# Reordering the last batch and the final stores of a fused cross-attention and squared-ReLU MLP kernel on one Trainium2 core

## The chip, the cores and the metric

The kernel runs on one core of one Trainium2 chip. The metric is the device time of one execution in microseconds (us). TensorE (PE) multiplies matrices into PSUM, VectorE (DVE) and ScalarE (ACT) do element-wise work and empty PSUM, GpSimd (POOL) and SyncE (SP) mostly issue DMA transfers here. The four runs of the kernel before took between 209.67 and 211.04 us, with a median of 210.51 us.

## What is computed

Eight batches, eight heads, 512 tokens and 32 state rows a head, 64 channels. Each token reads from the state, each state row reads from the tokens, and both reads pass through a two-layer MLP with a squared ReLU:

```python
scores = scale * np.matmul(x, state.transpose(0, 1, 3, 2))
a = softmax(scores)
xread = np.matmul(a, state)                # token reads, 512 rows a head
scores2 = scale * np.matmul(state, x.transpose(0, 1, 3, 2))
a2 = softmax(scores2)
sread = np.matmul(a2, x)                   # state reads, 32 rows a head
x = concat(xread, sread) -> [B * (512 + 32), 512]
h = x @ w_in                               # 512 -> 2048
r = np.maximum(h, 0.0)
g = s * (r * r) + b
out = g @ w_out                            # 2048 -> 512
```

The inputs and the output are float32; the kernel computes with float16 operands and float32 sums. The output has 4352 rows of 512.

## The kernel before

The work of a batch is laid out as a stage of sixteen steps, f = 0 to 15, one step for each block of 128 of the 2048 hidden channels. `pieces(s)` gives what stage s does beside that, and the main loop over s and f (lines 857 to 900) puts everything in order. The order on PE, SP and POOL is the order of the program (`manual_schedule`, line 691); a scheduler places VectorE's and ScalarE's instructions, with a few held behind others by `issue_after`.

**First layer.** The state is multiplied into `w_in` beforehand, so that a batch has a matrix M, built in four blocks by `att_M`, and h is the product of M with the shares `a4`. A step's h (`mm1_x`) is two matmuls of 512 columns into one bank of the PSUM pool `psH`, which has two buffers. ScalarE applies the ReLU (line 395), VectorE squares two steps at a time (line 402). The result g is held in float16.

**Second layer.** For batches 1 to 7 the second product is computed by a scheme with seven half-size products instead of eight, whose operands are sums and differences of blocks of g (`token_sum`) and of the output weights (`weight_sums`). `fast_items(b)` lists the small matmuls of these products in an order written by hand (lines 626 to 635). An entry (p, k0, k1) stands for product p, steps k0 to k1, two matmuls of 256 columns a step. Product 1 collects in bank A, and product 2 goes on collecting in bank A once product 1 has been read out as `qa` (line 585). Product 6 collects in bank B, is read out as `u2` (line 588, `u` in the profile), and product 7 goes on in B, until `u3` (line 593), and product 4 goes on in B. Products 5 and 3 share bank C. All three come from the pool `psO`, which has two buffers. The first half of product 6 needs the token sum number 2 of steps 0 to 3, its second half that of steps 4 to 7 (line 502).

A batch's first 16 matmuls (product 1) run in its own stage, the other 96 in the next stage, seven a step. In steps 4 to 12 of stages 2 to 7 these seven stand before that step's h (line 874), in the other steps behind it.

**Beside it.** In stage s the attention of batch s+1 is made: M and the scores T at step 4 and M again at step 10, the exponential E on ScalarE, its transpose ET by a DMA on SP, the shares on VectorE, and a transpose of these back (`a4`) by a DMA. T and M need the transposed state `stT`. For batches under NST = 5 the transpose is made on PE (`att_stT`, two matmuls of 128 columns and a copy on VectorE), for the others by one DMA transpose on SP (`stT_dma`, line 160), issued in step 9 of stage 2. V, the state read, is 32 small matmuls at step 10 (`att_V`, line 338) into a bank of `psH`, scaled by ScalarE. Its transpose goes into `srdT`; for the last batch PE makes it, at step 11 (`att_srT`).

**The end.** In stage 7, whose batch is the last, `mm1_sr(i)` for the state reads joins at steps 12 to 15: four matmuls of 256 columns into a bank of `psH`. Then lines 908 to 918 run the state reads' steps 4 to 15, with five of the last batch's remaining matmuls (`rest`) behind each, and two of the state reads' own (`rows`) from step 12 on. After that come the remaining products. In the last batch products 5 and 3 are done for each of two token blocks on its own, in a bank each, and `put_last` (line 569) adds up and stores each block: 128 rows of 256 float32, 128 KB.

Of the kernel before, what the change touches and what calls it, by code (L numbers as in the profile page):

```python
# [14 lines left out]
def kernel(  # L15
# [10 lines left out]
    nc = tc.nc  # L26
# [15 lines left out]
    FC = 512  # L42
    NFC = DF // FC
    NPE = 2
    NST = 5
    NDT = 3
    NH = DM // 2
    TH = S // 2
# [289 lines left out]
    def att_V(b):  # L338
        a = A[b]
        if b >= NDT - 1:  # L340
            ps = psH.tile([P, NG, D], FP32, tag="h", name=f"V_{b}")
        else:
            ps = att_ps([P, NG, D], FP32, f"V_{b}")
        for g in range(NG):
            for c in range(SCH):
                for q in range(NQ):
                    mm(
                        ps[32 * q : 32 * q + 32, g, :],
                        a["ET"][:, SCH * g + c, 32 * q : 32 * q + 32],
                        xn[b][:, head_of(g, q), chunk_of(c), :],  # L350
                        start=(c == 0),
                        stop=(c == SCH - 1),
                        tp=(0, 32 * q),
                    )
        a["sr"] = apool.tile([P, NG, D], FP16, name=f"sr_{b}", tag="sr")
        with tc.issue_after(G["relu"]):
            for g in range(NG):
                nc.scalar.mul(a["sr"][:, g], ps[:, g], a["rq"][:, g : g + 1])
# [7 lines left out]
    def att_srT(b):  # L366
        ps = att_ps([P, NQ, Ns], FP16, f"srT_{b}")
        mm(
            ps.rearrange("p q j -> p (q j)"),
            A[b]["sr"].rearrange("p g d -> p (g d)"),  # L370
            ident16,
            is_transpose=True,
        )
        nc.vector.tensor_copy(srdT[:, b], ps)
# [131 lines left out]
    def fast_items(b):  # L506
# [62 lines left out]
        def put_last(i):  # L569
            if not ends:  # L570
                ends.append(spare("osb_last"))
            osb = ends[0][:, i]
            nc.vector.scalar_tensor_tensor(
                osb, acc["C", i], s_bc, kept["u2"][:, i], ALU.mult, ALU.add
            )
            dst = out_BSn[b, 0:S].rearrange("(q ci cj) n -> cj ci q n", ci=2, cj=2)
            nc.sync.dma_start(dst[0][i][:, NH:DM], osb)

        def blk(n0):
            return bias_bc[:, n0 : n0 + NH].unsqueeze(1).broadcast_to([P, ni, NH])  # L580
# [42 lines left out]
            elif k == 7 and i == ni - 1:  # L623
                done(p)

        order = [(1, 0, 8), (6, 0, 4), (2, 0, 3), (6, 4, 8), (2, 3, 8), (7, 0, 8)]
        order += [(5, 0, 8), (4, 0, 8), (3, 0, 8)]
        if b == last_b:
            order = [(1, 0, 8), (6, 0, 4), (2, 0, 4), (6, 4, 8), (2, 4, 5)]
            order += [(7, 0, 8), (2, 5, 8), (4, 0, 8)]  # L630
        if b == "sr":
            order = [(p, 0, 8) for p in (1, 6, 2, 7, 5, 4, 3)]
        out = [(p, k, i) for p, k0, k1 in order for k in range(k0, k1) for i in range(ni)]
# [57 lines left out]
    with tc.manual_schedule(engines={ET.PE, ET.SP, ET.Pool}):  # L691
# [90 lines left out]
        def pieces(s):  # L782
            nb = s + 1
            out = {}

            def at(f, fn):
                out.setdefault(f, []).append(fn)

            def ahead(f, fn):
                out.setdefault((f, "ahead"), []).append(fn)  # L790

            if s == 1:
                at(0, lambda: att_xT_dma(2))
                at(0, gated_x3)
                at(0, lambda: att_ET(0))
                at(0, lambda: att_ET(1))
                at(8, lambda: att_xT_dma(3))
                at(12, lambda: load_x(4))
                at(2, lambda: att_M(1, 2, "act"))
                ahead(3, bias_sum)  # L800
                at(4, bias_end)
                at(3, lambda: att_M(1, 3, "act"))
                at(6, lambda: att_stT(2))
                at(10, bias_half)
                at(8, lambda: att_M(2, 0, "act"))
                at(8, lambda: att_M(2, 1, "act"))
                at(10, lambda: att_M(2, 2, "act"))
                at(10, lambda: att_T(2, [0, 1]))
                at(11, lambda: att_ET(2))
                at(12, lambda: att_D(2, [0, 1]))  # L810
                at(13, lambda: att_M(2, 3, "act"))
                at(13, lambda: att_V(0))
                return out
            if s == 2:
                at(1, lambda: load_x(5))
            elif s in (3, 4):
                at(1, lambda: load_x(s + 3))
            if nb < B:
                if nb < NST:
                    at(0, lambda: att_stT(nb))  # L820
                ahead(4, lambda: att_M(nb, 0, "later"))
                ahead(4, lambda: att_T(nb, [0, 1]))
                ahead(4, lambda: att_M(nb, 1, "later"))
                at(4, lambda: att_ET(nb))
                at(4, lambda: A[nb]["M", 0]())
                at(6, lambda: A[nb]["M", 1]())
                at(8, lambda: att_shares(nb))
                if s in (2, 3):
                    at(6, lambda: att_xT_dma(nb + 1))
                at(9, lambda: att_a4_dma(nb))  # L830
                if s == 2:
                    at(9, stT_dma)
                elif s in (3, 4):
                    at(9, lambda: att_xT_dma(s + 3))
            if s == 2:
                at(1, lambda: att_srT_dma(0))
                at(8, lambda: att_V(1))
                at(12, lambda: att_srT_dma(1))
            ahead(10, lambda: att_V(s))
            if nb < B:  # L840
                ahead(10, lambda: att_M(nb, 2, "later"))
                ahead(10, lambda: att_M(nb, 3, "later"))
                at(10, lambda: A[nb]["M", 2]())
                at(12, lambda: A[nb]["M", 3]())
            if s == last_b:
                at(11, lambda: att_srT(s))
            else:
                at(12, lambda: att_srT_dma(s))
            if s == last_b:
                for i in range(4):  # L850
                    at(12 + i, lambda i=i: mm1_sr(i))
            return out
# [4 lines left out]
        for s in range(1, B):  # L857
            todo_s = pieces(s)
            if s in fast:
                coming[s] = fast_items(s)  # L860
            first = coming[s][:16] if s in fast else []
            if s == 1:
                items = [[] for _ in range(NKF)]
                for f in [*range(5), *range(6, 14)]:
                    items[f] = [lambda u=todo.pop(0): unit(u)]
                items[14], items[15] = first[0:8], first[8:16]
            else:
                flat = coming[s - 1][16:] + first
                n = -(-len(flat) // NKF)
                items = [flat[n * f : n * f + n] for f in range(NKF)]  # L870
            for f in range(NKF):
                for fn in todo_s.get((f, "ahead"), []):
                    fn()
                if s > 1 and 4 <= f < 13:
                    for fn in items[f]:
                        fn()
                    items[f] = []
                mm1_x(s, f)
                if s > 1 and f in (4, 5):
                    with tc.issue_after(G["last"]):  # L880
                        token_sum(s - 1, 4, f - 4)
                if s in fast:
                    if f in ((7, 9) if s == 1 else (7, 11)):
                        with tc.issue_after(G["last"]):
                            token_sum(s, 3, f // 8)
                    if s == 1 and f in (13, 14):
                        with tc.issue_after(G["last"]):
                            token_sum(s, f - 12, 0)
                    if s > 1 and f in (11, 12):
                        token_sum(s, f - 10, 0)  # L890
                    if f == 15:
                        token_sum(s, 1, 1)
                        token_sum(s, 2, 1)
                for fn in todo_s.get(f, []):
                    fn()
                if s == 1 and 5 <= f < 13:
                    with tc.issue_after(G["last"]):
                        sums.pop(0)()
                for fn in items[f]:
                    fn()  # L900
# [3 lines left out]
        def go(items, n):  # L904
            for _ in range(n):
                items.pop(0)()

        for f in range(4, NKF):
            mm1_sr(f)
            if f in (4, 5):  # L910
                token_sum(last_b, 4, f - 4)
            if f in (5, 9):
                token_sum("sr", 3, f // 8)
            if f in (11, 12, 13):
                token_sum("sr", (1, 2, 4)[f - 11], 0)
            go(rest, 5)
            if f >= 12:
                go(rows, 2)
        go(rest, 4)
# [37 lines left out]
```

## Time and profile before

| | |
|---|---|
| median of four runs | 210.51 us |
| the profiled execution | 210.34 us |
| its span, first to last instruction | 208.6 us |
| granted TensorE clock, mean | 0.994 |
| PE matmul, busy | 199.3 us (96%) |
| DVE busy | 160.0 us (77%) |
| ACT busy | 126.7 us (61%) |
| steady stages 3 to 6, from one stage's step 4 to the next one's | 21.1 us, and 21.7 once |

A stage's span holds about 21 us of PE work. PE's busy time overlaps from one matmul to the next, so a share of 96% tells that PE hardly rests, but not how much of the time it could save; for that the starts of the matmuls are compared. Waits of an engine that is ahead of PE cost nothing: ScalarE waits 46.6 us in all for h, at intervals of at most 1.4 us.

The last DMA issues and what they move, from the page: the two last stores of 128 KB on SP landed a median of 2.3 us after their issue, and the DMA transpose `stT_all`, issued at 70.8 us, landed after 4.3 us.

### The profile page before, as it was taken

What the parts mean: (1) busy time and instruction counts of PE and PEld (TensorE: products, weight loads), DVE (VectorE), ACT (ScalarE), POOL (GpSimd) and SP (SyncE); (2) the same over time, 40 slices, a digit from 0 to 9 for tenths busy, and PEclk for the clock granted to TensorE, in tenths of its full rate; (3) what the DMA queues carried; (4) which work ended last, traced back from release to release, by engine and by line L of the source; (5) the groups of instructions that cost most, each with busy time, mean ns of one, the idle gap of its engine ahead of it and who ended that gap; (6) DMA issues with size and microseconds to landing.
All of it is one profiled execution on the core that took longest, in us unless ns stands there. A gap on an engine that the chain in (4) does not pass through costs nothing.

```text
span 208.6 us, 4792 instructions
## 1 busy us (share of the span) xinstructions
PE 199.3 (96%) x1949; PEld 130.0 (62%) x1949; DVE 160.0 (77%) x275; ACT 126.7 (61%) x252; POOL 37.7 (18%) x64
## 2 busy tenths in 40 slices
PE   7988999999999999999999999999999999999991
PEld 2433343445666776677666666676667776878880
DVE  1587826979759985999579977997799787696861
ACT  3678864799477757775776567666767355533100
POOL 5970001411110231023101210210021102100210
PEclk9999999999999999999999999999999999999997
DMA  6999995999998694949752924250415012100242
GB/s 192 220 200 206 207 191 87 186 166 174 184 166 175 154 159 68 179 110 206 106 95 68 178 68 101 72 139 3 101 61 149 0 53 101 53 2 0 97 125 86
DMA packets 46491, 25.49 MB, mean 122 GB/s; under 512 B 31428, under 2 KB 44484, under 8 KB 46468
## 3 DMA queue, kind: packets, MB, share of 16 engines
q0 software_dynamic: 15536, 16.19, 40.3%
q1 hardware_dynamic: 30132, 8.62, 23.9%
q10 hardware_dynamic: 800, 0.36, 0.7%
q8 instruction: 15, 0.25, 0.5%
q14 instruction: 8, 0.07, 0.1%
HBM read 17.33 MB, written 8.91 MB: 126 GB/s over the span
## 4 chain that ended last, share of the span: by engine, by line
PE 74%; DMA 10%; DVE 8%; ACT 3%; issue 2%; POOL 0%; SPq 0%
PE h L70 21%; PE oB L70 15%; PE oC L70 10%; PE oA L70 9%; PE o L70 7%; DMA xT<-xn 5%; PE Mps L70 4%; DMA ET<-E 3%; DMA xf<-in_x_dram 3%; PE h_sr L70 2%; ACT r L395 2%; DVE g L402 2%; PE oB_sr L70 1%; PE T L70 1%; PE V L70 1%
## 5 line engine op out<-in xcount | busy, mean ns | idle before, releaser
L395 ACT ACTIVATE r<-h 128x512 f16<-128x512 f32 x126 | 74.4, 602 | 47.4 <-PE h L70 46.6
L70 PE MATMUL h<-a,M 128*128 128x512 f16 x256 | 74.2, 379 | 1.2 <-DVE M L320 0.6
L402 DVE TENSOR_TENSOR g<-r 128x1024 f16<-128x1024 f16 x64 | 43.5, 682 | 16.2 <-ACT r L395 15.6
L70 PEld LDWEIGHTS <-s 128*128 128x128 f16 x448 | 43.3, 98 | 17.5 <-DVE s L502 1.9
L70 PEld LDWEIGHTS <-g 128*128 128x128 f16 x400 | 37.6, 98 | 21.0 <-issue 5.3
L567 POOL DMA_DIRECT2D out_dram<-osb x27 | 18.2, 675 | 125.7 <-DVE osb L559 79.1
L70 PE MATMUL oB<-wd,s 128*128 128x256 f16 x224 | 32.6, 273 | 0.3 <-DVE u L588 0.2
L70 PEld LDWEIGHTS <-M 128*128 128x128 f16 x256 | 24.5, 98 | 12.9 <-issue 1.8
L70 PE MATMUL oA<-wo,g 128*128 128x256 f16 x224 | 31.7, 273 | 0.1
L297 ACT CAST M<-Mps 128x1024 f16<-128x1024 f32 x20 | 20.1, 1007 | 0.0
L70 PE MATMUL oC<-wd,s 128*128 128x256 f16 x112 | 16.5, 273 | 0.0
L70 PE MATMUL o<-wo,g 128*128 128x512 f16 x64 | 16.3, 380 | 0.0
L70 PE MATMUL oB<-wd,g 128*128 128x256 f16 x112 | 15.9, 273 | 0.0
L70 PE MATMUL oC<-wo,s 128*128 128x256 f16 x112 | 15.3, 273 | 0.0
L395 ACT ACTIVATE r_sr<-h_sr 128x256 f16<-128x256 f32 x16 | 6.1, 382 | 8.7 <-PE h_sr L70 8.7
L234 ACT ACTIVATE E<-T 128x256 f16<-128x256 f32 x20 | 7.4, 383 | 4.7 <-PE T L70 4.7
L588 DVE SCALAR_TENSOR_TENSOR u<-oB,s_bc,qa 128x512 f32<-128x512 f32 x7 | 5.3, 751 | 6.1 <-PE oB L70 6.1
L502 DVE TENSOR_TENSOR s<-s,g 128x1024 f16<-128x1024 f16 x14 | 9.6, 684 | 0.2
L70 PE MATMUL h_sr<-srdT,wi 128*128 128x256 f16 x64 | 9.6, 273 | 0.0
L496 DVE TENSOR_TENSOR s<-g 128x1024 f16<-128x1024 f16 x14 | 9.6, 684 | 0.0
L504 DVE TENSOR_TENSOR s<-g,s 128x1024 f16<-128x1024 f16 x14 | 9.6, 684 | 0.0
L500 DVE TENSOR_TENSOR s<-g,g 128x1024 f16<-128x1024 f16 x14 | 9.6, 683 | 0.0
(107 smaller groups left out, 205.6 us busy)
## 6 DMA issues: line engine op xcount, KB each, us to landing
out_dram<-osb POOLq DMA_DIRECT2D x31, 256.0 KB, 3.7
xn<-in_x_dram POOLq DMA_DIRECT2D x7, 512.0 KB, 9.4
wi<-in_moe_w_in_dram POOLq DMA_DIRECT2D x4, 512.0 KB, 8.8
wo<-in_moe_w_out_dram POOLq DMA_DIRECT2D x4, 512.0 KB, 16.4
xf<-in_x_dram SPq DMA_DIRECT2D x2, 512.0 KB, 4.6
out_dram<-osb_sr SPq DMA_DIRECT2D x8, 32.0 KB, 1.5
out_dram<-osb_sr ACTq DMA_DIRECT2D x8, 32.0 KB, 1.7
out_dram<-osb_last SPq DMA_DIRECT2D x2, 128.0 KB, 2.3
```

Of the source, the lines that this page charges most:

```text
L70: return nc.tensor.matmul(out, lhsT, rhs, start=start, stop=stop, tile_position=tp, is_transpose=is_transpose, skip_group_check=True,)
L234: nc.scalar.activation(a["E"][:, g, 256 * m : 256 * m + 256], Ts[m][:, g, :], AF.Exp, scale=scale, accum_out=a["rs"][:, NG * m + g : NG * ...
L297: nc.scalar.copy(dst, ps)
L395: nc.scalar.activation(r16[:, f % 2], hps, AF.Relu)
L402: nc.vector.tensor_mul(gt[:, f % 4 - 1 : f % 4 + 1], r16, r16)
L496: nc.vector.tensor_sub(o, a11, a21)
L500: nc.vector.tensor_add(o, a21, a22)
L502: nc.vector.tensor_sub(o, SQ[b, 1, j], a11)
L504: nc.vector.tensor_sub(o, a12, SQ[b, 2, j])
L567: nc.gpsimd.dma_start(dst[j][:, :, n0 : n0 + NH], osb)
L588: nc.vector.scalar_tensor_tensor(u, acc["B"], s_bc, kept["qa"], ALU.mult, ALU.add)
```

## The change

Six edits, in the order of the file:

- NST is 4 instead of 5: batch 4's state is transposed by the DMA too, which then moves eight blocks instead of six.
- `put_last` issues the first of the two last stores on ScalarE's queue, and the second in two halves of 64 rows, one on SP and one on ScalarE's queue.
- In ordinary batches the second product's first part, which stands between the two halves of the sixth, has four steps instead of three, and its second part four instead of five.
- In the last batch that first part has three steps instead of four; then come the sixth product's second half, three steps of the second product (instead of one), the seventh product, and the last two (instead of three).
- In stage 7 the state read V of the last batch is made ahead of step 4 instead of 10, its transpose at step 6 instead of 11, and the seven small matmuls of a step stand behind that step's h in all steps.
- In the state reads' steps 4 to 15 the number of small matmuls behind each is 4, 3, 5, 5, 5, 5, 5, 5, 5, 6, 6, 6 instead of 5 each.

```diff
-    NST = 5
+    NST = 4
...
             dst = out_BSn[b, 0:S].rearrange("(q ci cj) n -> cj ci q n", ci=2, cj=2)
-            nc.sync.dma_start(dst[0][i][:, NH:DM], osb)
+            if i == 0:
+                nc.scalar.dma_start(dst[0][i][:, NH:DM], osb)
+                return
+            for eng, p in ((nc.sync, 0), (nc.scalar, P // 2)):
+                eng.dma_start(dst[0][i][p : p + P // 2, NH:DM], osb[p : p + P // 2])
...
-        order = [(1, 0, 8), (6, 0, 4), (2, 0, 3), (6, 4, 8), (2, 3, 8), (7, 0, 8)]
+        order = [(1, 0, 8), (6, 0, 4), (2, 0, 4), (6, 4, 8), (2, 4, 8), (7, 0, 8)]
         order += [(5, 0, 8), (4, 0, 8), (3, 0, 8)]
         if b == last_b:
-            order = [(1, 0, 8), (6, 0, 4), (2, 0, 4), (6, 4, 8), (2, 4, 5)]
-            order += [(7, 0, 8), (2, 5, 8), (4, 0, 8)]
+            order = [(1, 0, 8), (6, 0, 4), (2, 0, 3), (6, 4, 8), (2, 3, 6)]
+            order += [(7, 0, 8), (2, 6, 8), (4, 0, 8)]
...
-            ahead(10, lambda: att_V(s))
+            ahead(4 if s == last_b else 10, lambda: att_V(s))
...
             if s == last_b:
-                at(11, lambda: att_srT(s))
+                at(6, lambda: att_srT(s))
...
-                if s > 1 and 4 <= f < 13:
+                if 1 < s < last_b and 4 <= f < 13:
...
-            go(rest, 5)
+            go(rest, (4, 3, 5, 5, 5, 5, 5, 5, 5, 6, 6, 6)[f - 4])
```

## The prediction

> **What bounds the kernel now.** I read the page's engine line first, then the chain of waits, then TensorE's timeline from 100 us on, matmul by matmul, and for each hole the timeline of VectorE and ScalarE beside it; last the DMA issues at the end and at 70 us.
>
> The page, engine line and the chain's shares by engine:
>
> ```profile
> PE 199.3 (96%) x1949; PEld 130.0 (62%) x1949; DVE 160.0 (77%) x275; ACT 126.7 (61%) x252; POOL 37.7 (18%) x64
> ...
> PE 74%; DMA 10%; DVE 8%; ACT 3%; issue 2%; POOL 0%; SPq 0%
> ```
>
> TensorE (PE) is the bound: three quarters of the chain is its own work. A matmul's duration on the page (273 ns for 256 columns) is longer than its slot, because matmuls overlap; start to start in one block the trace gives 109 ns for 256 columns and 216 ns for 512. With these slots a block's end is computable, and whatever lies between it and the next start is a hole. After 58 us PE loses little outside five places: one in stage 5 (batch 5, 118 to 124 us) and four in the last batch and the state-read stage. Timeline of PE, one line a block (start us, duration us, tiles, count, idle time and releaser where recorded):
>
> ```profile
> 119.33 0.59 PE L70 MATMUL h<-a,M 128*128 128x512 f16 x2
> 120.01 0.94 PE L70 MATMUL oB<-wd,s 128*128 128x256 f16 x7
> ...
> 175.45 0.60 PE L70 MATMUL h_sr<-srdT,wi 128*128 128x256 f16 x4
> 176.30 0.59 PE L70 MATMUL h<-a,M 128*128 128x512 f16 x2 [0.25 <-ACT r L395]
> ...
> 182.61 0.49 PE L70 MATMUL oB<-wd,s 128*128 128x256 f16 x3
> 183.16 0.38 PE L70 MATMUL oA<-wo,g 128*128 128x256 f16 x2
> ...
> 186.76 0.27 PE L70 MATMUL oA<-wo,g 128*128 128x256 f16 x1
> 187.22 0.60 PE L70 MATMUL oB<-wd,s 128*128 128x256 f16 x4 [0.19 <-DVE u L588]
> ...
> 191.26 0.49 PE L70 MATMUL oA<-wo,g 128*128 128x256 f16 x3
> 191.75 0.38 PE L70 MATMUL oB<-wd,g 128*128 128x256 f16 x2
> ```
>
> The reader is to see, line by line: 119.33 + 2 x 0.216 = 119.76, next start 120.01, hole 0.25; 175.45 + 4 x 0.109 = 175.89 to 176.30, 0.41; 182.61 + 0.33 = 182.94 to 183.16, 0.22; 186.87 to 187.22, 0.35; 191.59 to 191.75, 0.16. The last four add to 1.14 us.
>
> What VectorE (DVE) did at two of those holes, and the last stores:
>
> ```profile
> 182.37 0.74 DVE L585 SCALAR_TENSOR_TENSOR qa<-oA,s_bc,bias_bc 128x512 f32<-128x512 f32 x1
> 183.03 0.68 DVE L502 TENSOR_TENSOR s<-s,g 128x1024 f16<-128x1024 f16 x1
> ...
> 186.42 0.75 DVE L588 SCALAR_TENSOR_TENSOR u<-oB,s_bc,qa 128x512 f32<-128x512 f32 x1
> ...
> 203.74 1.26 SPq L577 DMA_DIRECT2D out_dram<-osb_last  x2
> 203.96 0.48 DVE L573 SCALAR_TENSOR_TENSOR osb_last<-oC,s_bc,u 128x256 f32<-128x256 f32 x1 [0.39 <-PE oC L70]
> ```
>
> qa ends at 183.11, just ahead of oA at 183.16; u ends at 187.17, just ahead of oB at 187.22. So these holes are PSUM banks being emptied.
>
> **What the Trainium skill says.** "TensorE: Matmul & The Clock Gate", section "Wait — 56ns, not 53.3ns?": a warm matmul of N columns takes N over 2.4 GHz plus about 2.5 ns from start to start, 215.7 ns for 512. The trace agrees (216, and 109 for 256). Same page, "Step-by-step: what each phase is for": matmuls stay in program order and only weight loads are pulled ahead. The trace agrees in that each hole stalls all that follows; so what counts is which matmul stands next when a bank is late. "DMA: Bandwidth & Descriptors", "Issuing engines are not separate DMA queues": two issuing queues share the same DMA engines and save only issue time. No run here shows two halves of a store yet. Same page, "Anatomy of one DMA — SWDGE (gpsimd) path": a fixed cost near 2.0 us, mostly the write's receipt, for the GpSimd path. Of the two last stores, on SP, one landed 1.9 us after its issue, the other 2.8.
>
> **The change part by part.**
>
> (1) h ahead of the products in the last batch, V at step 4, transpose at step 6. PE work is the same: the 32 V matmuls cost 0.35 us plus about 0.2 us of switching wherever they stand. In steps 4 to 12 each h comes one block of seven products (0.76 us) earlier. At step 12 the order was h(12), h_sr(0), h(13); an h bank comes free 0.43 (two h matmuls) + 0.20 + 0.60 (ScalarE's relu row) + 0.02 = 1.25 us after the h starts, and only 0.87 us of work stood between. Now h(12), h_sr(0), seven products, h(13): 1.63 us. Hole of 0.41 gone. New waits: V takes an h bank at step 4. It waits for relu(h2), done 0.06 us after h3 starts, well before V; h4 waits for relu(h3), 1.25 after h3 starts, and starts 1.66 after; h5 waits for V's two scalings (ScalarE, 0.51), done at about 2.4, and starts at 2.85. Behind the scalings on ScalarE stands relu(h4), delayed by some 0.1, and h6 wants it 1 us later. The 0.23 us copy of the state read moves forward on VectorE, where u3 behind it is wanted near 3 us after p7 ends. Cost nothing; if a cover failed, 0.1 to 0.3.
>
> (2) Last batch, 3-5 split and 3-3-2 for the second product, and 4, 3, 5 ... items a step. I count from the end of p1 (181.19 in before). oA (p2) stood 1.75 after it and waited for qa, ready at 1.97; now h_sr, 4 oB, h_sr, 3 oB, h_sr, 1 oB stand before it: 2.20. Hole 0.22 gone. The sixth product's second half wants the token sum ready at 2.52 and starts at 3.3. It ends at 4.6 (5.0 before); u waits behind other VectorE work that before ended at 5.18, so u is out at 5.9 to 6.0. The seventh product now starts at 4.6 + two h_sr + 6 oA = 6.15. Hole 0.35 gone, slack 0.2. Fourth product: the seventh now ends two small matmuls later, 1.1 us before the fourth starts, against 1.3; u3 needs 0.2 + 0.75, and VectorE now does one more small sum (0.42) before it, which the order of the built program shows. In my count that sum is done 0.3 us before the seventh product ends. Hole 0.16 gone, with only 0.1 slack. Sum of (1) and (2): 1.14 us; between 0.6 and 1.14.
>
> (3) 4-4 split in ordinary batches. Two second-product matmuls (0.22 us) go in front of the sixth product's second half, which gives its token sum that long. In stages 2, 3, 4 and 6 PE has no hole there: gain nothing. In stage 5 the hole of 0.25 shrinks to 0.03: gain 0.22. u2 comes 0.22 later; VectorE idles 0.98 us before it at 163.72, and so waits longer; behind it stand a squaring, a sum and an eviction that end 1.06 us before the next needed squaring in that stage. The seventh product follows far behind. Cost nothing; between 0 and 0.25 gain, since the stage 5 hole comes from a late transpose (ET landed 6.5 us after issue, others near 4.8) that may differ by execution.
>
> (4) NST 5 to 4. Two PE transposes (56 ns each, 0.11 us) and one VectorE copy (285 ns, beside PE) go in stage 3; stT_all grows from six blocks to eight. SP's issue of six took 1.30 us and of eight (ET, a) 1.23 to 1.26, so the queue behind it, two srdT transposes, is not moved. Landing was at 75.0; two blocks more I estimate at 4.3 x 8/6 = 5.7, so 76.5. First use is batch 4's M at 79.2. Gain 0.11.
>
> (5) Last stores. First store on ACT's queue, free at 203.72, against an issue at 203.74: no change. Second in halves on SP and ACT, both free. Fixed cost stays; the half's descriptors are out sooner (the data packets of a 128-row store ran over 0.45 us). I take 0.2. The bounds: ACT's own issue could add 0.1; the second store landed at 2.8 only because two instruction fetch packets of 8 KB (0.76 us each, at 205.3 and 205.6) lay before its last packets, and 14 of 16 engines had reported by 206.6. If the fetches fall elsewhere, 0.8 more goes.
>
> Sum: 1.14 + 0.22 + 0.11 + 0.2 = 1.67. The profiled execution took 210.34 us (span 208.57, 1.77 outside it), which gives 208.67; the median of the four runs is 0.17 higher, 210.51, so 208.84, say 208.8 us.
>
> **The rivals.**
>
> A, the waits move. VectorE has no idle time from 180.8 to 187.1, the reordering takes no work from it, and the slack I found after u and u3 is 0.2 and 0.1. For it: that saturation. Against: qa and u were each just behind PE, by 0.2 to 0.35, and are pushed past by more. Then only the 0.41, 0.11, half of (3) and of (5), and some 0.15 of (2) are gained: 0.9, 209.6 us.
>
> B, the last store misses the fetches: 0.8 more, 208.0 us. For: 14 engines on time. Against: fetches come at the end of each program, and halves use the same engines.
>
> C, slower: stT_all lands late. Batch 4's M and T now wait for that transpose. Behind it PE's whole queue waits, with E, ET and the shares for the next stage. For: the srdT transposes issued just after it took 4.1 and 5.2 us as the next x load began (75 to 79 us), and an srdT in stage 4 took 8.0. Against: 2.7 us of slack by my estimate. It costs from 79.2 on; it makes up for all the gains at a landing near 80.5 (1.2 of wait and 0.6 of VectorE backlog as in stage 4), and at 82 gives 2.8 + 0.6 - 1.6 = 1.8 slower, 212.3.
>
> That the change does nothing: not likely, as the built order shows every move.
>
> **How the numbers follow.** Forecast 0.68, A 0.18, B 0.08, C 0.06. The forecast's own range from the bounds is 208.1 to 209.3. A lies inside 209.9, so I take 207.9 to 209.8, leaving out C and tails. About 0.5% (1.05 us) is what a measurement of this kernel can tell from no change: the limit is 209.46. Forecast and B lie below it almost wholly, A mostly above: faster 0.75, same 0.19, slower 0.06.
>
> **What would show it.** h(13) starts without a ScalarE releaser; no hole above 0.05 before oA after p1, before p7 and before p4; in stage 5 the oA pair between h(2) and oB; in stage 3 no stTps, and M for batch 4 with no DMA releaser; last landing some 1.7 us earlier. I am wrong if the same holes stand before p7 or p4, if PE waits at about 79 us, or if the last landing does not follow PE's end.

## The result

The changed kernel takes 209.74 us (median of 43 runs, 208.91 to 210.84), beside 210.25 us of the kernel before (64 runs on the same chips). The ratio is 0.9975, with a 95% interval of 0.9964 to 0.9986. So it is about 0.5 us faster, where 1.67 were forecast.

The profiled execution took 209.25 us, with a span of 207.5. Its engine line and the chain's shares by engine, on its page:

```profile
PE 197.3 (95%) x1947; PEld 130.1 (63%) x1947; DVE 159.9 (77%) x274; ACT 126.8 (61%) x252; POOL 38.0 (18%) x64
...
PE 89%; DVE 3%; DMA 3%; ACT 2%; issue 0%; POOL 0%; ACTq 0%
```

PE's share of the chain has grown from 74% to 89%. Part of that is a start that went otherwise; from 58 us on it is waits that are gone from the path. Timeline of PE at the four places in the last batch and the state reads (start us, duration us, what, count):

```profile
174.85 0.60 PE L70 MATMUL h_sr<-srdT,wi 128*128 128x256 f16 x4
175.28 0.93 PE L70 MATMUL oC<-wo,s 128*128 128x256 f16 x7
176.05 0.59 PE L70 MATMUL h<-a,M 128*128 128x512 f16 x2
...
183.02 0.27 PE L70 MATMUL oB<-wd,s 128*128 128x256 f16 x1
183.13 0.60 PE L70 MATMUL oA<-wo,g 128*128 128x256 f16 x4
...
186.95 0.27 PE L70 MATMUL oA<-wo,g 128*128 128x256 f16 x1
187.06 0.60 PE L70 MATMUL oB<-wd,s 128*128 128x256 f16 x4
...
190.99 0.60 PE L70 MATMUL h_sr<-srdT,wi 128*128 128x256 f16 x4
191.43 0.82 PE L70 MATMUL oB<-wd,g 128*128 128x256 f16 x6
```

With 0.109 us a matmul every block starts where the one before it ends: 175.28 + 0.76 = 176.04, 183.02 + 0.11 = 183.13, 186.95 + 0.11 = 187.06, 190.99 + 0.44 = 191.43. All four holes are gone, and from T of batch 7 to the start of the last matmul it is 59.11 us (143.56 to 202.67) instead of 60.25 (143.40 to 203.65): 1.14 us, to the hundredth what the holes added to.

Then why only 0.5 us? Two other places of the trace after differ. The first is SP's timeline in stage 3, where the shares of batch 4 are transposed for the next stage. Before, then after:

```profile
91.13 1.24 SPq L290 DMA_TRANSPOSE a<-aT  x1
92.46 4.19 SPq L204 DMA_TRANSPOSE xT<-xn  x1
```

```profile
91.87 1.83 SPq L290 DMA_TRANSPOSE a<-aT  x1
93.80 3.61 SPq L204 DMA_TRANSPOSE xT<-xn  x1
```

The same transpose takes 0.6 us longer to issue, and by its semaphore it lands 4.31 us after its issue instead of 3.24. h of batch 4 wants it at 96.25 us; it lands at 96.18. This execution just escapes a wait. The second place is the end, in the view of the tile `osb_last`:

```profile
L578 ACTq DMA_DIRECT2D out_dram<-osb_last x1: 381/381/381, 202.8 to 202.8; - x1
L581 SPq DMA_DIRECT2D out_dram<-osb_last x1: 557/557/557, 203.5 to 203.5; - x1
L581 ACTq DMA_DIRECT2D out_dram<-osb_last x1: 583/583/583, 203.5 to 203.5; - x1
```

A half takes 557 and 583 ns to issue (a whole store 356 to 388 ns), and the halves land 2.30 and 2.59 us after their issue.

The two profiles taken alone would mislead. The start differs between executions (the first load of `stf` landed after 3.8 us in one and 5.7 us in the other, and the first T came at 6.43 and 8.05 us). From T of batch 3 to the end the one execution after is even 1.97 us shorter than the one before (148.76 and 150.73 us), more than was forecast: it escapes the wait in stage 3, and the execution before had the latest ET of stage 4 of all sixteen traces, with 0.58 us of holes behind it. The medians have to decide, and the experiments have to tell where the rest went.

### The profile page after: what moved, and what is told of

It reads as the page before. It is cut to its first block, busy times and chain, and to the rows that moved or that the text cites. A ratio compares the mean times of both kernels' runs of the same rounds, so it can differ in the third digit from the quotient of the medians.

```text
span 207.5 us, 4788 instructions
## 1 busy us (share of the span) xinstructions
PE 197.3 (95%) x1947; PEld 130.1 (63%) x1947; DVE 159.9 (77%) x274; ACT 126.8 (61%) x252; POOL 38.0 (18%) x64
## 4 chain that ended last, share of the span: by engine, by line
PE 89%; DVE 3%; DMA 3%; ACT 2%; issue 0%; POOL 0%; ACTq 0%
PE h L70 25%; PE oB L70 18%; PE oA L70 12%; PE oC L70 12%; PE o L70 7%; PE Mps L70 4%; PE h_sr L70 3%; DMA stf<-in_state_dram 3%; PE V L70 1%; PE oB_sr L70 1%; ACT r L395 1%; PE T L70 1%; DVE M L320 1%; PE oA_sr L70 1%; PE oC_sr L70 1%; PE wsum_ps L70 0%
## 5 line engine op out<-in xcount | busy, mean ns | idle before, releaser
L70 PE MATMUL oA<-wo,g 128*128 128x256 f16 x224 | 32.5, 273 | 0.0
```

Source lines behind the costliest of these rows:

```text
L70: return nc.tensor.matmul(out, lhsT, rhs, start=start, stop=stop, tile_position=tp, is_transpose=is_transpose, skip_group_check=True,)
```

## The experiments

Theory S: the split of the last store costs. Theory D: what is gained early is lost again to the pace of the transfers. Theory W: the waits of the last batch come back in most executions. After the first four runs two more: F, PE's instruction fetch has moved into the shares' transpose, and Q, the longer `stT_all` has set that transpose back. Each trace is one execution; an experiment's ratio rests on 5 to 22 runs. The times at the end of this section stand beside runs of the kernel before on the same chip.

**The parts, each alone or left out.** First the whole change without its store edit (e1), against the changed kernel:

```diff
-            if i == 0:
-                nc.scalar.dma_start(dst[0][i][:, NH:DM], osb)
-                return
-            for eng, p in ((nc.sync, 0), (nc.scalar, P // 2)):
-                eng.dma_start(dst[0][i][p : p + P // 2, NH:DM], osb[p : p + P // 2])
+            nc.sync.dma_start(dst[0][i][:, NH:DM], osb)
```

> The change with its store edit undone: both last stores whole, on SP, as in the kernel before. Theory S (the split costs: the halves landed 2.30 and 2.59 us after their issue, a whole store that no fetch packet hits about 1.95): faster than the kernel before by 1.0 to 1.4 us, ratio 0.993 to 0.995, and the last store lands near 1.9 to 2.0 us after its issue in most executions. Theory D (early gains are swallowed by the pace of the transfers, the split is neutral or a gain): ratio 0.9975 as for the whole change, or up to 0.999. Theory W (the waits of the last batch come back in most executions): ratio 0.997 to 0.999 too, with holes in PE's timeline before p2, p7 or p4 of the last batch.

Ratio 0.9924 (0.9899 to 0.9950), against 0.9975 with the edit: S, though the last store landed after 2.28 us and not 1.9 to 2.0. The opposite, the store edit alone on the kernel before (e2):

> The store edit alone on the kernel before. Theory S: slower by 0.3 to 0.7 us, ratio 1.0015 to 1.0035, landings near 2.3 and 2.6 us. Theories D and W: no change or up to 0.2 us faster, ratio 0.999 to 1.000.

1.0013 (1.0002 to 1.0025), 0.3 us slower, just short of the range of S; the halves landed after 2.79 and 2.98 us. The last batch's edits alone (e3: its order, its counts, V, its transpose, and h first):

```diff
-            order = [(1, 0, 8), (6, 0, 4), (2, 0, 4), (6, 4, 8), (2, 4, 5)]
-            order += [(7, 0, 8), (2, 5, 8), (4, 0, 8)]
+            order = [(1, 0, 8), (6, 0, 4), (2, 0, 3), (6, 4, 8), (2, 3, 6)]
+            order += [(7, 0, 8), (2, 6, 8), (4, 0, 8)]
...
-            ahead(10, lambda: att_V(s))
+            ahead(4 if s == last_b else 10, lambda: att_V(s))
```

> The edits of the last batch alone (h ahead of the products, V at step 4, its transpose at step 6, the last batch's order and its counts), with NST = 5, the ordinary order and whole stores. Theories S and D: 1.1 us faster (0.41 + 0.22 + 0.35 + 0.16), ratio 0.994 to 0.9955, since nothing of the transfers' pace lies behind 165 us. Theory W: 0.4 to 0.7 us, ratio 0.997 to 0.998, with holes left in the last batch.

0.9932 (0.9910 to 0.9954), 1.4 us, with 1.1 inside the interval. W falls: in all ten traces with these edits PE takes 59.11 us from T of batch 7 to the start of the last matmul, in the six without 60.25 or 60.38. NST = 4 and the 4-4 split alone (e4):

> NST = 4 and the 4-4 split alone. Theory D: nothing, ratio 0.9995 to 1.0005, or slower where stT_all is late (then PE waits at about 79 us before M of batch 4). Theories S and W: 0.1 to 0.3 us faster, ratio 0.9985 to 0.9995.

1.0005 (0.9988 to 1.0021): no gain to be seen, though the interval reaches into both forecasts. The trace tells more. PE waited 0.75 us before h of batch 4, not at 79 us before its M. D's place was wrong: `stT_all` landed at 75.8 us, in time. In all kernels with NST = 4 up to here the shares' transpose of stage 3 landed after 4.3 to 5.1 us, in those with NST = 5 after 3.2.

**What delays that transpose.** The trace has packets of 16 KB on a DMA queue of their own, each about 1 us long, 15 in an execution, marked as instruction fetches. That they are PE's is read from e5 and e6, where adding or leaving out PE instructions moves them. In the kernel before one starts at 90.2 us, 0.9 us ahead of the transpose's issue; in the changed one at 92.3 us, 0.4 us behind it. The two removed transposes are four PE instructions (with their weight loads), so a block of PE's program ends at another place of the work. (Why four instructions move this fetch by 1.3 us is not shown.) e5 is e4 with four PE instructions put back that do nothing useful:

```diff
+    def pad_pe():
+        ps = att_ps([P, 2, P], FP16, "pad_ps")
+        for n in range(2):
+            mm(ps[:, n, :], st16[:, 8 + n].rearrange("p k d -> p (k d)"), ident16, is_transpose=True)
...
+                if nb == NST:
+                    at(0, pad_pe)
```

> NST = 4 and the 4-4 split, with two PE transposes that nobody reads put where the two removed ones were in stage 3, so that PE's instructions stand where they stood in the kernel before; stT_all still moves eight blocks. In the three kernels with NST = 4 so far, the shares' transpose of stage 3 (a<-aT issued near 91 to 93 us) took 1.8 to 2.0 us to issue and 4.3 to 5.1 us to land; in the three with NST = 5, 1.24 and 3.1 to 3.2. Theory F (four PE instructions fewer move PE's instruction fetch, a 16 KB packet of about 1 us on one DMA engine, from just before that transpose into it): issue 1.23 and landing 3.1 to 3.3 us again, fetch before the issue, no wait of h of batch 4; ratio 0.998 to 1.000. Theory Q (the longer stT_all itself leaves the transpose queue behind): still 1.8 to 2.0 and 4.2 to 5.1; ratio 1.000 to 1.002.

Fetch at 90.2 us again, issue 1.23 us, landing after 3.23 us, no wait, ratio 0.9967 (0.9952 to 0.9982): faster than e4 with more work on PE. SP's line:

```profile
91.14 1.23 SPq L295 DMA_TRANSPOSE a<-aT  x1
```

e5 is also 0.7 us faster than the kernel before, more than F gave. In the traces this is stage 5, from its holes (21.10 us from T of batch 5 to T of batch 6, instead of 21.68), and the end (3.78 us from the last eviction to the last instruction, instead of 4.13); both come back below. And the other way round, four PE instructions fewer in the kernel before (e6):

```diff
-        warm_up(11)
+        warm_up(9)
```

> The kernel before with two of its first eleven warm-up matmuls left out (they write a bank that nobody reads), so four PE instructions fewer from the start, NST = 5, stT_all of six blocks. Theory F: the fetch in stage 3 falls into the shares' transpose, issue 1.8 to 2.0 us and landing 4.2 to 5.1, and in some executions PE waits before h of batch 4; time 0 to 0.5 us longer, ratio 1.000 to 1.0025. Theory Q: issue 1.24, landing 3.1 to 3.2, ratio 0.999 to 1.001.

Fetch 0.4 us behind the transpose's issue, issue 2.08 us, landing after 5.68 us, and the time is 1.0031 (1.0010 to 1.0051) of before: 0.65 us lost by leaving out two idle matmuls (the traced execution, 211.83 us, is 1.0 above this kernel's median). SP's line, and PE's line of h of batch 4 with its releaser:

```profile
91.42 2.08 SPq L290 DMA_TRANSPOSE a<-aT  x1
...
97.14 0.60 PE L70 MATMUL h<-a,M 128*128 128x512 f16 x2 [1.17 <-DMA a<-aT]
```

The view of windows says what the transfers did in between. Columns: stretch in us and its length, busy time of PE, PEld, DVE, ACT and POOL, granted clock, share of the DMA engines, GB/s. Before, then e6:

```profile
93.20:94.20 1.00, 1.00 (x9) 0.71 (x8) 1.00 (x2) 1.00 (x3) 0.00 (x0) 1.00 0.95 234
```

```profile
93.20:94.20 1.00, 1.00 (x10) 0.71 (x8) 1.00 (x3) 1.00 (x2) 0.00 (x0) 1.00 1.21 15
```

The packets that start in this microsecond take as much of the DMA engines' time (share 0.95 and 1.21), yet next to nothing moves: 15 GB/s where 234 went. Twenty of the transpose's 256-byte packets, begun from 93.10 to 93.37 us, last 1.1 to 1.4 us each. F stands by two edits in opposite directions (e5 also puts a PSUM buffer back in its turn, e6 touches none); Q falls, since e5 moves eight blocks and e6 six. All sixteen traces agree: in eleven the fetch starts 0.5 to 1.1 us ahead of the issue, and the transpose lands after 3.2 us; in the five with four PE instructions fewer (the change, e1, e4, e6, e12) it starts 0.3 to 0.6 us behind the issue, and the landing is at 4.3 to 5.7. How the fetch holds the transpose up is not shown: in e6 its own packet is recorded from 91.86 to 93.01 us, so it had ended when the long packets began.

**Which part of the store edit.** e7, NST = 5 with the last batch's edits and the 4-4 split, asks whether the split of the second product costs anything:

> The last batch's edits and the 4-4 split, with NST = 5 and whole stores on SP: the change without the two edits that gave nothing. Theory S and F: the gain of the last batch alone (ratio 0.9932) or up to 0.2 us more, ratio 0.992 to 0.9945. If the 4-4 split was what cost in the run with NST = 4 and 4-4: 0.995 to 0.997.

0.9940 (0.9922 to 0.9958), not to be told from e3; a difference of 0.6 us either way could hide in the intervals. e8 moves the first store only:

```diff
-            nc.sync.dma_start(dst[0][i][:, NH:DM], osb)
+            (nc.scalar if i == 0 else nc.sync).dma_start(dst[0][i][:, NH:DM], osb)
```

> The kernel before with only the first of the two last stores moved to ScalarE's queue, the second whole on SP. Theory S (it is the halves): no change, ratio 0.9990 to 1.0005, the second store's engines report at 1.95 us after issue, two late ones where a fetch lies in the way. If ScalarE's queue as such costs (its later end, or its own fetch): slower by 0.2 us or more, ratio above 1.001.

Neither: 0.9972 (0.9953 to 0.9990), 0.6 us faster. The trace has it:

```profile
203.33 0.48 DVE L573 SCALAR_TENSOR_TENSOR osb_last<-oC,s_bc,u 128x256 f32<-128x256 f32 x1 [0.39 <-PE oC L70]
203.84 0.36 SPq L577 DMA_DIRECT2D out_dram<-osb_last  x1
```

From the end of the second eviction to the last instruction it is 3.46 us, and 4.13 before. With SP free, the second store's issue starts 0.03 us after its eviction ends (203.81 to 203.84 us) instead of 0.20 (204.45 to 204.65). And it lands after 2.27 us instead of 2.76: the first of the two 8 KB instruction fetches at the end starts 1.42 us after its issue, not 0.62, and delays it less. That is no accident of this trace: e9 has the same 1.42, and the other three traces with NST = 5 and both stores whole on SP (e3, e6, e7) have 0.62 to 0.65.

**Both losses taken out, one by one and together.** All four are the whole change or near it: e9 is e7 with e8's stores; e10 has the unread transposes and e8's stores; e11 only the unread transposes; e12 only e8's stores.

> NST = 5, the last batch's edits, the 4-4 split, the first last store whole on ScalarE's queue and the second whole on SP. If the parts add as measured alone (0.994 for the last batch with 4-4, 0.9972 for the first store on ScalarE's queue): ratio 0.990 to 0.993, and PE's fetch stays before the shares' transpose of stage 3 (issue 1.24, landing 3.1 to 3.3). If the gain of the store on ScalarE's queue came from where the fetches at the end fell in that kernel alone: 0.993 to 0.995.

> The whole change, but the second last store whole on SP, and two PE transposes that nobody reads in place of the two removed in stage 3. Theories S and F together: both losses taken out, ratio 0.989 to 0.992; shares' transpose of stage 3 lands after 3.1 to 3.3 us, no hole before h of batch 4.

> The whole change with the two unread transposes only; halves kept. Theory F: 0.3 to 0.8 us faster than the whole change, ratio 0.993 to 0.996, transpose at 3.1 to 3.3 us, halves near 2.3 and 2.6 us. If the fetch was not what cost: ratio 0.997 to 0.998 as the whole change.

> The whole change, but the second last store whole on SP (the first stays on ScalarE's queue); no padding. Theory S: 0.3 to 0.9 us faster than the whole change, ratio 0.993 to 0.996, last store near 1.95 to 2.3 us after issue; shares' transpose of stage 3 still 4.2 us or more (theory F). If the halves were not what cost: 0.997 to 0.998.

The unread transposes bring 0.9975 to 0.9946 and 0.9908 to 0.9878, 0.6 us each time; whole stores bring 0.9975 to 0.9908 and 0.9946 to 0.9878, 1.4 us each time. By the intervals each of these four differences is uncertain by 0.4 to 0.7 us. Both losses are there, and as far as that tells they add. e12 shows the one that is left in it, on PE's timeline:

```profile
94.27 0.59 PE L70 MATMUL h<-a,M 128*128 128x512 f16 x2
...
96.06 0.61 PE L70 MATMUL h<-a,M 128*128 128x512 f16 x2 [0.43 <-DMA a<-aT]
```

and the end with and without halves (e10, then e11; first the eviction of the second block, then the issues):

```profile
202.30 0.48 DVE L578 SCALAR_TENSOR_TENSOR osb_last<-oC,s_bc,u 128x256 f32<-128x256 f32 x1 [0.39 <-PE oC L70]
202.82 0.36 SPq L582 DMA_DIRECT2D out_dram<-osb_last  x1
```

```profile
202.46 0.48 DVE L578 SCALAR_TENSOR_TENSOR osb_last<-oC,s_bc,u 128x256 f32<-128x256 f32 x1 [0.39 <-PE oC L70]
202.97 0.56 SPq L586 DMA_DIRECT2D out_dram<-osb_last  x1
202.97 0.57 ACTq L586 DMA_DIRECT2D out_dram<-osb_last  x1
```

The whole store lands 1.94 us after its issue, the later half 2.59. That is 0.65 us in the traces against 1.4 in the times. By the packets of the traces the whole store's first data move 0.86 us after its issue, those of the halves 1.20 us (SP) and 1.49 us (ScalarE's queue) after theirs. e2 and e8, too, differ by the split alone, with NST = 5: 0.9 us in the times, 0.7 in the traces. Two more runs looked at the rest, both the change with the unread transposes, e13 with the halves one behind the other on SP:

```diff
-            for eng, p in ((nc.sync, 0), (nc.scalar, P // 2)):
-                eng.dma_start(dst[0][i][p : p + P // 2, NH:DM], osb[p : p + P // 2])
+            for p in (0, P // 2):
+                nc.sync.dma_start(dst[0][i][p : p + P // 2, NH:DM], osb[p : p + P // 2])
```

> The whole change with the two unread transposes, and both halves of the second last store issued on SP, one behind the other. If what costs is the issue of two halves at the same moment on two queues: the issues take 0.36 us again, the halves land near 1.9 us after their own issue, the second issued 0.4 to 0.9 us after the first; ratio between the whole store (0.9878) and the halves on two queues (0.9946), about 0.990 to 0.992. If splitting costs wherever it is issued: 0.994 to 0.996.

> The whole change with the two unread transposes and the halves on two queues, once more, to have it beside the halves on SP: ratio 0.993 to 0.996, halves landing near 2.3 and 2.6 us. If the difference of 1.4 us to the whole store was in part that of two groups of runs: up to 0.992.

e13: 0.9938 (0.9915 to 0.9962); e14: 0.9926 (0.9897 to 0.9955). Halves on one queue are no better, and each still takes 0.56 to 0.59 us to issue: it is the splitting, not the meeting of two queues. e14 repeats e11 and puts the price at 1.0 us (0.9926 against 0.9878), so part of the 1.4 may be scatter between groups of runs. Whether it is truly more than the 0.65 us of the traces, and why, stays open.

| kernel | ratio to before (95%) | shares' transpose of stage 3 lands after, us | last store lands after, us | last eviction to last instruction, us |
|---|---|---|---|---|
| before | 1 | 3.24 | 2.76 | 4.13 |
| the change | 0.9975 (0.9964 to 0.9986) | 4.31 | 2.59 | 4.01 |
| e1 whole stores on SP | 0.9924 (0.9899 to 0.9950) | 4.82 | 2.28 | 3.84 |
| e2 store edit alone | 1.0013 (1.0002 to 1.0025) | 3.23 | 2.98 | 4.17 |
| e3 last batch alone | 0.9932 (0.9910 to 0.9954) | 3.23 | 2.79 | 4.16 |
| e4 NST, 4-4 alone | 1.0005 (0.9988 to 1.0021) | 5.09 | 2.40 | 3.99 |
| e5 e4 and unread transposes | 0.9967 (0.9952 to 0.9982) | 3.23 | 2.19 | 3.78 |
| e6 two warm-up matmuls fewer | 1.0031 (1.0010 to 1.0051) | 5.68 | 2.82 | 4.15 |
| e7 e3 and 4-4 | 0.9940 (0.9922 to 0.9958) | 3.22 | 2.79 | 4.15 |
| e8 first store on ACT | 0.9972 (0.9953 to 0.9990) | 3.25 | 2.27 | 3.46 |
| e9 e3, 4-4, e8 | 0.9888 (0.9861 to 0.9915) | 3.23 | 2.16 | 3.35 |
| e10 change, unread transposes, e8 | 0.9878 (0.9853 to 0.9904) | 3.23 | 1.94 | 3.36 |
| e11 change, unread transposes | 0.9946 (0.9931 to 0.9960) | 3.23 | 2.59 | 4.01 |
| e12 change, e8 | 0.9908 (0.9889 to 0.9926) | 4.93 | 1.97 | 3.38 |
| e13 halves on SP | 0.9938 (0.9915 to 0.9962) | 3.21 | 2.30 | 4.25 |
| e14 e11 again | 0.9926 (0.9897 to 0.9955) | 3.25 | 2.60 | 4.01 |

e9 and e10 beat both kernels: e10 at 207.52 us (six runs), by 2.6 us the kernel before on its chip (0.0122 x 210.36).

**The end, with NST = 5 and 4.** In the seven traces with NST = 5 both 8 KB fetches at the end start 0.6 to 1.8 us after the second store's issue. In the nine with NST = 4 only one does; the other starts 0.3 to 0.4 us after the last instruction. With both stores whole on SP the last landing is then at 2.19 to 2.40 us instead of 2.76 to 2.82, and the stretch from the last eviction to the last instruction is 0.1 to 0.4 us shorter (3.78 to 3.99, 4.13 to 4.16); with the first store on ScalarE's queue it is the same (3.36 and 3.38, 3.46 and 3.35). e5 has PE's instructions back and still only one fetch, so PE's count does not decide this; which of the other instructions that went does was not tested.

## Why the prediction was right and wrong

**Parts (1) and (2), 1.14 us: right**, by mechanism and size. All four holes closed, also the two where I found only 0.1 and 0.2 us of slack; PE's stretch at the end is 59.11 us in every trace with these edits, and alone they gave 1.4 us, with 1.1 in the interval. Rival A did not come: qa, u and u3 were pushed past, and none was late again.

**Part (3), 0.22 us: there in the traces, too small for the times, and not by the forecast's way.** From T of batch 5 to T of batch 6 PE takes 21.10 us in all eleven traces with the 4-4 split, and 21.17 to 21.68 in the five without. But the ET issued in that stretch lands 5.28 to 5.87 us after its issue in the eleven, and 5.96 to 6.48 in the five, where the excess over 21.10 is each time ET's landing less 5.9 us. By that, no hole would have been left in the eleven even without the 0.22 us of work put in front. The split itself brought ET's landing forward (e7, with the split, 5.46; e3, without, 6.02), which I had not seen coming, and why it does is open. In the times e3 and e7 differ by less than their intervals.

**Part (4), gain 0.11 us: the fetch costs about 0.6 us that the part did not have.** The 0.11 us on PE is there: in the traces without a late start or unread transposes, T of batch 3 to T of batch 4 takes 21.55 us with NST = 4 and 21.66 to 21.68 with 5. The step that failed is the count of what goes with the two removed transposes: I priced PE's time, VectorE's copy and the blocks of `stT_all`, and put the place of PE's instruction fetches at nothing. One of them moved into a transpose on which the next stage waits. "The queue behind it ... is not moved" was right as far as `stT_all` goes (its issue took 1.33 us, not 1.30; Q fell). That it landed at 76.45 us, where 76.5 was forecast, is luck: it took 4.83 us, not 5.7, and was issued 0.8 us later than in the kernel before. Rival C looked at the transposes, and at the wrong one: `stT_all` was in time. The forecast also missed the fetch that leaves the end. What NST = 4 is worth in all is not resolved: e1 against e7 gives a gain of 0.3 us, e12 against e9 a loss of 0.4, each uncertain by 0.7.

**Part (5), gain 0.2 us: wrong, and in sign.** The step that failed is the sentence "the half's descriptors are out sooner". A half takes 0.56 us to issue against 0.36, its first data move 0.3 us later or more (1.20 and 1.49 us after the issue against 0.86), and it lands 0.65 us later than a whole store; by the times the split costs 0.9 to 1.4 us. "First store on ACT's queue: no change" was wrong the other way: alone that edit gave 0.6 us, and the trace has it: the second store is issued 0.17 us sooner after its eviction and lands 0.5 us sooner after its issue, less delayed by the fetches. The sentence of the Trainium skill that I quoted ("DMA: Bandwidth & Descriptors", "Issuing engines are not separate DMA queues": two issuing engines save only issue time) should have made me take no gain for the halves. The runs agree in so far as halves on two queues are no faster than on one (0.9926 and 0.9946 against 0.9938); that splitting costs issue time is what they add.

**The sum.** 1.14 from (1) and (2), 0.6 from the first store on ScalarE's queue, less 0.9 to 1.4 for the halves, less 0.6 for the fetch (this is net of the 0.11 us saved on PE), gives a loss of 0.3 to a gain of 0.2 us; with e3's measured 1.4 us in place of 1.14, up to 0.5. Stage 5 (0.1 to 0.6 us in the traces) and the fetch that leaves the end (0.16 us between e2 and the change) come on top. The measured gain is 0.5 (0.3 to 0.8): the parts carry intervals of 0.3 to 0.7 us each, and the sum agrees within them. Rival B did happen in a form: with whole stores the last landing is at 1.94 to 2.8 us, according to how many fetches lie at the end and where.

## What to carry to other kernels

On a path where a DMA transpose is awaited, removing instructions from another engine can cost time: its instruction fetches are DMA packets too, and they move when the program's length does, so look in the trace for where they lie against the awaited transfers before and after an edit. Closing holes by putting ready work ahead of a late bank was worth, on PE's timeline, just what the holes added to. A last store of 128 rows was best issued whole here, on a queue that had nothing else to issue just then.

## What the runs showed of the hardware

- With a 16 KB instruction fetch of about 1 us that began 0.3 to 0.6 us behind the issue of a DMA transpose, that transpose landed after 4.3 to 5.7 us instead of 3.2, and its issue on SP took 1.8 to 2.1 us instead of 1.23; a fetch 0.5 to 1.1 us ahead of the issue did nothing. The Trainium skill ("Runtime: NRT & Kernel Launch", "Instruction fetch mechanics") calls the cost of crossing a block mostly hidden; here it was 0 to 1.3 us of PE's time, by its place.
- A store of 64 rows of 1 KB took 0.55 to 0.59 us to issue, one of 128 rows 0.36 to 0.39 and one of 32 rows 0.31 to 0.44, on either queue.
- The 8 KB fetches at the end of the program (0.3 to 0.95 us) delayed one or two of the sixteen engines of the last store, if they came early enough: in the kernel before fourteen had reported at 1.96 us, the last at 2.76. With NST = 4 one of the two came after the end, in all nine traces.
